# Column-norm attention and two MoE layers: three shared buffers, a shorter norm sum, and a new plan for the first groups

## Chip, cores and metric

One core of one Trainium2 chip. The metric is the device time of one execution in microseconds, the median of several runs. The engines are TensorE (PE: matmuls; PEld: its weight loads), VectorE (DVE), ScalarE (ACT), GpSimd (POOL, hardly used here) and SyncE (SP), which issues every DMA of this kernel.

## The reference

Cut to what matters (6016 tokens, 256 channels, hidden width 2048):

```python
qn = q / (np.linalg.norm(q, axis=1, keepdims=True) + 1e-06)   # norms over the 6016 tokens
kn = k / (np.linalg.norm(k, axis=1, keepdims=True) + 1e-06)
s = kn.transpose(0, 2, 1) @ qn / tau                          # 256 x 256
a = np.exp(s - s.max(-1, keepdims=True))
a /= a.sum(-1, keepdims=True) + 1e-09
x = v @ a                                                     # 6016 x 256
g = np.maximum(x @ w_in1, 0.0) ** 2;  x = g @ w_out1          # first layer
h = x @ w_in2
g = np.maximum(0.01 * h, h);          out = g @ w_out2        # second layer
```

All of it is in 32-bit floats. The weights reach the kernel as 64-bit numbers, which it converts itself.

## The kernel before, in words

**Splitting.** A product in full precision is made from three matmuls: each operand is split into a rounded high part and a low part (`split`, `low`, L137 to L142), and high x high, high x low and low x high are summed in PSUM (`mm3`, L572).

**Attention (L344 to L533).** q and k are read in 14 groups of 1, 2, ten times 4, 3 and 1 row tiles, five groups ahead. For each tile, TensorE accumulates the transposed scores `sT` (L423). For the norms, ScalarE squares a group (`square`, L386) and VectorE adds the squares of the groups of four into `acc` (`accumulate`, L400); after the last of them it adds `acc`'s four parts into `sums_`. The squares of the last two groups (3 and 1 tiles) are not added. At the end, `norm_sums` (L373) lets TensorE sum over partitions with matmuls of one column, four for each 512 columns: three times for the last-but-one group, once for `sums_`, once for the last group. A matmul of 32-bit floats shows as two records. From `pn` follow the norms (square root on ScalarE, a chain of small instructions on VectorE), the scaled scores `sTs`, their transposes `s`, maximum and exponential, the transposed exponentials `eT` with their split, and then `fold(0)`. `keep_warm` puts matmuls without a use between these.

**Fold (L270).** The first layer's input weights are multiplied by the attention matrix once, so that v itself can be the layer's input: `fold(g)` is 12 matmuls into bank `c`; `fold_high` (ScalarE) and `fold_low` (VectorE) scale and split the result into the tile `wi` of group g.

**Weights (`Unit`, L156).** A unit is 256 rows or columns of one weight matrix. Its steps are load (SP), exponent (VectorE), rebias (ScalarE), mantissa, mantissa_low, sign, high (VectorE), round (ScalarE), low (VectorE), store (SP). `first_i` are w_in's units 0 and 1, `first_o` is w_out's unit 0, `others` the rest of the first layer. In the attention the generators `steps_i` and `steps_o` hand out VectorE's steps one by one (`run`); the steps of ScalarE and the last subtraction are collected in `later` and put out where `flush(ACT)` or `flush(DVE)` stands.

**Layers.** The tokens are six blocks p of two halves of 512 (one of 448); the hidden width is eight groups g of 256. Group by group, `first` or `product` makes the hidden values, relu and square (or the leaky form) and the cast are ScalarE's, the low part is VectorE's, and `second` adds the product with w_out to the block's outputs `y`. Block 0 of layer 1 uses the function `plain`, all others `strassen`. After a block, `y_done` copies the two halves of `y` into a buffer `o` (`take`) and sends it off (`put`): to DRAM for the second layer, or to the output. `o` has one buffer in layer 1 (tag "o") and shares the two of `v` in layer 2 (tag "v"). `load_v` (L247) reads a half block of v in four DMAs.

**Order.** Every engine works strictly in the order in which its instructions are written. In the attention that order is the program's. After it, a planner collects `(time, function)` pairs in `plan` and writes them out sorted by time (L980). One plan unit is a matmul of 512 columns. `at` sets a time, `on` also reserves an engine, `fit` takes the first gap of an engine that is long enough (`Gaps`). The times of the first groups are in `PLAIN`, one dictionary each: `first`, `relu`, `square`, `cast`, `low`, `fold`, `fold_high`, `fold_low` and `second` are times from the group's start, `length` is the time to the next group, and `stretch` multiplies the times. The third dictionary holds for group 2 and all later groups of `plain`. `convert` (L829) fits the remaining weight units into the gaps.

Of the kernel before, what the change touches and what calls it, by code (L numbers as in the profile page):

```python
# [50 lines left out]
def attn_moe_moe2(  # L51
# [40 lines left out]
    def in_order(x):  # L92
        return x.rearrange("p (q k c) -> p k q c", q=Q, k=KC)

    def ordered(x):
        return x.rearrange("p (k q c) -> p k q c", q=Q, k=KC)
# [1 line left out]
    const = ctx.enter_context(tc.tile_pool(name="const", bufs=1))  # L98
    wpool = ctx.enter_context(tc.tile_pool(name="wpool", bufs=2))
    cpool = ctx.enter_context(tc.tile_pool(name="cpool", bufs=2))  # L100
    vpool = ctx.enter_context(tc.tile_pool(name="vpool", bufs=2))
    xpool = ctx.enter_context(tc.tile_pool(name="xpool", bufs=2))
    dram = ctx.enter_context(tc.tile_pool(name="dram", bufs=1, space=DRAM))
    ps_h = ctx.enter_context(tc.tile_pool(name="ps_h", bufs=1, space=PSUM))
# [210 lines left out]
    def flush(engine):  # L315
        steps, later[engine] = later[engine], []
        for step in steps:
            step()
# [18 lines left out]
    def run(steps, n):  # L337
        for _ in range(n):
            next(steps, None)
# [4 lines left out]
    with (  # L344
# [28 lines left out]
        def norm_sums(src, first=False, last=False):  # L373

            for b in range(4):
                x = src[:, b * P : (b + 1) * P]
                nc.tensor.matmul(  # L377
                    pn[:, b : b + 1], x, ones, start=first and b == 0, stop=last, skip_group_check=True
                )
# [6 lines left out]
        def square(n, t):  # L386
            g = groups[n][1]
            flat = t.rearrange("p g a c -> p g (a c)")
            if n == whole[0]:
                nc.scalar.activation(acc, flat, AF.Square)  # L390
                return
            squares[n] = att2.tile([P, G, 2 * C], F32, tag="sq", name="sq")
            if n <= whole[-1]:
                nc.scalar.activation(squares[n][:, :g], flat[:, :g], AF.Square)
                return
            nc.scalar.activation(squares[n][:, :g, :C], flat[:, :g, :C], AF.Square)
            for i in range(g):
                nc.scalar.activation(ordered(squares[n][:, i, C:]), in_order(flat[:, i, C:]), AF.Square)

        def accumulate(n):  # L400
            if not whole[0] <= n <= whole[-1]:
                return
            for i, at in ((0, 0), (1, 1)) if n == whole[0] else ((n, 0),):
                sq, g = squares.pop(i), groups[i][1]
                tt(acc[:, at : at + g], acc[:, at : at + g], sq[:, :g], op=ALU.add)
            if n == whole[-1]:
                tt(acc[:, 0:2], acc[:, 0:2], acc[:, 2:4], op=ALU.add)
                a0, a1 = acc[:, 0], acc[:, 1]
                tt(sums_[:, :C], a0[:, :C], a1[:, :C], op=ALU.add)
                tt(ordered(sums_[:, C:]), in_order(a0[:, C:]), in_order(a1[:, C:]), op=ALU.add)  # L410

        for n, (t0, g) in enumerate(groups):
            t = qk.pop(n)
            last_group = n == NS - 1
            flush(ACT)
            square(n, t)
            if last_group:
                nc.scalar.activation(small[:, 7, 0:1], ones, AF.Sqrt)
            accumulate(n - 1)
            flush(DVE)  # L420
            for i in reversed(range(g)):
                for j in range(KC):
                    nc.tensor.matmul(  # L423
                        sT[j][:, :C],
                        t[:, i, 0, j * P : (j + 1) * P],
                        t[:, i, 1],
                        start=n == 0 and i == g - 1,
                        stop=last_group and i == 0,
                    )
            if n == 1:  # L430
                for u in first_i:
                    u.load()
            if W0 <= n < W0 + 4:
                run(steps_i, 2)
            elif W0 + 4 <= n < W0 + 6:
                run(steps_i, 1)
            if n + AHEAD < NS:
                load_qk(n + AHEAD)
            elif n + AHEAD == NS:
                load_v(0, 0)  # L440
                first_o.load()
                nc.sync.dma_start(tau_sb, tau.partition_broadcast(P))
                load_v(0, 1)
            if n == W0 + 7:
                for u in others[:2]:
                    u.load()
        for i in range(3):
            norm_sums(squares[NS - 2][:, i], first=i == 0)
        norm_sums(sums_)
        norm_sums(squares[NS - 1][:, 0], last=True)  # L450
        run(steps_o, 2)
        flush(ACT)
        nc.vector.reciprocal(rtau, tau_sb)
        y, m, z, r = (small[:, i] for i in range(4))
        nc.scalar.activation(y, pn[:, :4], AF.Sqrt, bias=tiny, scale=0.25)
# [11 lines left out]
        sTs = [att.tile([P, C], F32, name=f"sTs{j}") for j in range(KC)]  # L467
        ts(ordered(sTs[0]), in_order(sT[0][:, :C]), r[:, 0:1], rtau, op0=ALU.mult, op1=ALU.mult)
        nc.scalar.activation(ordered(sTs[1]), in_order(sT[1][:, :C]), AF.Copy, scale=rq1)
        run(steps_o, 1)  # L470
        s = [bank("e", "s0"), bank("y3", "s1")]

        xs = att2.tile([P, 4, 512], F32, tag="sq", name="xs")
# [21 lines left out]
        for i in range(KC):  # L495
            nc.vector.reduce_max(mx[:, i], s[i][:, :C], axis=AX.X)
            ts(nb[:, i], mx[:, i], rk[:, i : i + 1], -1.0, op0=ALU.mult, op1=ALU.mult)
            nc.scalar.activation(
                e[i], s[i][:, :C], AF.Exp, bias=nb[:, i], scale=rk[:, i : i + 1], accum_out=sm[:, i]
            )  # L500
        x_transpose(0, 0)
        x_transpose(1, 0)
        for i in range(KC):
# [23 lines left out]
        x_high(2)  # L527
        x_low(1)
        x_low(2)
        run(steps_o, 3)  # L530
        flush(ACT)
        flush(DVE)
        first_o.store()  # L533


    gpool = ctx.enter_context(tc.tile_pool(name="gpool", bufs=4))
# [13 lines left out]
    def fit(engine, t, cost, fn, *args):  # L550
# [6 lines left out]


    PLAIN = [
        dict(first=(0, 6, 18.4, 24.4), fold=12, second=(), length=36, relu=(6.4, 12.4, 26.9, 34.2), stretch=1,  # L560
             square=(18, 36.9), cast=(29.6, 44.4), low=(34.7, 49.5), fold_high=22.6, fold_low=27),
        dict(first=(0, 6, 12, 18), fold=24, length=50, relu=(5.6, 13, 20.4, 30.6), stretch=1,
             second=((30.4, (1, 0, 0)), (36.4, (1, 0, 1)), (42.4, (1, 1, 0))),
             square=(15.7, 37.6), cast=(26, 42.2), low=(31.1, 47), fold_high=33.3, fold_low=39),
        dict(first=(0, 12, 30.4, 42.4), fold=24, length=62, stretch=1.14, relu=(6.4, 18.4, 36.8, 48.8),
             second=((6, (2, 1, 1)), (18, (1, 0, 0)), (36.4, (1, 0, 1)), (48.4, (1, 1, 0))),
             square=(21.2, 51.6), cast=(25.4, 55.8), low=(30.2, 60.6), fold_high=31, fold_low=37),
# [36 lines left out]
    def y_done(t, n, half):  # L604

        L, p, _ = units[n]
        w = WIDTH[p]
        key = L, p, half
        if key == (2, NP - 1, 1):
            at(t, finish_last)  # L610
            return
        o = {}

        def take(d):
            ys = y_t[key]
            if d == 0:

                o[0] = vpool.tile([P, 16, C // Q], F32, name="o", **({"tag": "v"} if L == 2 else {"tag": "o", "bufs": 1}))
            if L == 2:
                nc.vector.transpose(  # L620
                    o[0][:, : w // B, d * B : (d + 1) * B], ys[d][:, :w].rearrange("p (g t) -> p g t", t=B)
                )
                return
            to = o[0].rearrange("p g c -> p (g c)")[:, d * w : (d + 1) * w]
            (nc.scalar.copy if d == 0 else nc.vector.tensor_copy)(to, ys[d][:, :w])

        def put():
            if L == 2:
                for b, to in enumerate(blocked(out, p, half)):
                    nc.sync.dma_start(to, o[0][b * B : (b + 1) * B, : w // B])  # L630
                return
            for d in range(KC):
                from_ = o[0].rearrange("p g c -> p (g c)")[:, d * w : (d + 1) * w]
                nc.sync.dma_start(x2_d[p][:, SLOT[d, half], :w], from_)

        t0 = fit(DVE if L == 2 else ACT, t, 3.1 if L == 2 else 2.7, take, 0)
        t1 = fit(DVE, max(t, t0 - 3) if L == 1 else t0 - 0.5, 3.1, take, 1)
        at(max(t0, t1), put)
# [42 lines left out]
    def plain(n, t0):  # L681

        L, p, g = units[n]
        w = WIDTH[p]
        m = PLAIN[min(n, 2)]
        T = lambda x: t0 + m["stretch"] * x
        x_at = {(0, 0): (2, 0), (0, 1): (2, 1), (1, 1): (1, 0), (1, 0): (1, 1)}

# [116 lines left out]
    start, lengths, now = [], [], 0  # L805
    for n in range(LAST + 1):
        L, p, g = units[n] = n // (NP * NG) + 1, n // NG % NP, n % NG
        lengths.append(PLAIN[min(n, 2)]["length"] if n < NG else 45 * (WIDTH[p] + 32) / 544)
        start.append(now)
        now += lengths[-1]  # L810

    for n in range(LAST + 1):
        (plain if n < NG else strassen)(n, start[n])

# [51 lines left out]
    for i, u in enumerate(others):  # L866
        end = convert(u, 0, i < 2)
        n, x = (u.g - 1, "fold") if u.kind == "i" else (u.g + 1, "second")
        m = PLAIN[min(n, 2)]
        due = start[n] + m["stretch"] * (m[x] if u.kind == "i" else 18)  # L870
        assert end < due, (u.kind, u.g, end, due)
        if u.kind == "i":
            used["whl"][-1] = due + 8
# [139 lines left out]
```

## Time and profile before

| | |
|---|---|
| median of 3 runs | 1063.73 us (1063.1 to 1064.23) |
| profiled execution, its own time | 1062.22 us |
| its span, first to last instruction | 1060.3 us |
| TensorE busy | 1042.3 us, 98% of the span |
| VectorE, ScalarE busy | 786.8 us (74%), 715.8 us (68%) |
| mean granted clock of TensorE | 0.994 of 2.4 GHz |

Times in the trace count from the start of the span. Matmuls are pipelined and their ends are modelled, so a group's end can lie after the start of the next. A busy share is a mean over stages with different limits; what counts is which wait ends last in a stage.

### The profile page before, as it was taken

To read this page: it belongs to the slowest core of one execution; us is meant where nothing else is said; L and a number is where in the kernel's file an instruction comes from. 1 tells how busy PE (TensorE), PEld (TensorE's weight loads), DVE (VectorE), ACT (ScalarE), POOL (GpSimd) and SP (SyncE) were. 2 spreads that over 40 slices of the span, in tenths; PEclk is the share of its full clock that TensorE was granted. 3 is DMA by queue.
4 is the path that set the end of the run, shared out by engine and by line. 5 is a ranking of instruction groups with operands and counts; after the bars stand their busy time and mean duration, and the time that the engine had idled before them with its cause. 6 is when DMAs were issued, how large, how long until landed. Compare 5 with 4: busy or idle time off the path is not lost.

```text
span 1060.3 us, 12864 instructions
## 1 busy us (share of the span) xinstructions
PE 1042.3 (98%) x4798; PEld 881.1 (83%) x4798; DVE 786.8 (74%) x1096; ACT 715.8 (68%) x854; POOL 0.7 (0%) x6
## 2 busy tenths in 40 slices
PE   8989999999999999999998999999999999999998
PEld 6978888888888788998887888888888888998887
DVE  4788988887988888888886756866765765866554
ACT  5568887888888887887886655655655654655543
POOL 0000000000000000000000000000000000000000
PEclk9989999999999999999999999999999999999999
DMA  9937548558558658758466435544543634644431
GB/s 330 275 116 201 185 164 207 180 208 196 222 218 260 226 202 267 225 223 312 155 223 243 148 130 197 160 160 181 172 164 147 200 138 175 203 164 158 152 147 40
DMA packets 118590, 203.48 MB, mean 192 GB/s; under 512 B 52608, under 2 KB 66176, under 8 KB 116864
## 3 DMA queue, kind: packets, MB, share of 16 engines
q1 hardware_dynamic: 118528, 202.66, 56.6%
q8 instruction: 38, 0.62, 0.2%
q14 instruction: 24, 0.20, 0.1%
HBM read 165.15 MB, written 37.49 MB: 191 GB/s over the span
## 4 chain that ended last, share of the span: by engine, by line
PE 92%; DMA 3%; DVE 2%; issue 1%; SPq 1%; ACT 1%; DVEq 0%; ACTq 0%
PE y L574 43%; PE hc L574 11%; PE ha L574 10%; PE hb L574 10%; PE he L574 5%; PE sT L423 4%; PE h L574 4%; PE y L592 2%; DMA v<-in_v_dram 1%; DMA x<-o 1%; PE pw L278 1%; DVE c L763 1%; PE pn L377 1%; PE warm L135 0%; DMA wst<-in_moe_w_in_dram 0%
## 5 line engine op out<-in xcount | busy, mean ns | idle before, releaser
L574 PE MATMUL y<-g,wo 128*128 128x512 f32 (+1 forms) x2208 | 551.6, 385 | 0.0
L574 PEld LDWEIGHTS y<-g,wo 128*128 128x128 f32 x2208 | 414.6, 188 | 77.3
L138 DVE TENSOR_TENSOR g<-c,g 128x1024 fp32r<-128x1024 f32 (+1 forms) x192 | 230.4, 1200 | 28.0 <-ACT g L662 22.3
L662 ACT CAST g<-c 128x1024 fp32r<-128x1024 f32 (+1 forms) x192 | 198.8, 1035 | 4.5
L671 ACT ACTIVATE c<-c 128x1024 f32<-128x1024 f32 (+1 forms) x96 | 100.3, 1045 | 141.0 <-DVE c L763 141.0
L574 PE MATMUL hc<-x,wi 128*128 128x512 f32 (+1 forms) x528 | 146.7, 386 | 5.0 <-DVE c L763 4.9
L574 PE MATMUL hb<-x,wi 128*128 128x512 f32 (+1 forms) x528 | 146.6, 386 | 0.3 <-DVE c L763 0.3
L574 PE MATMUL ha<-x,wi 128*128 128x512 f32 (+1 forms) x528 | 146.9, 387 | 0.0
L574 PEld LDWEIGHTS hc<-x,wi 128*128 128x128 f32 x528 | 98.6, 188 | 25.1 <-DVE c L763 7.2
L574 PEld LDWEIGHTS hb<-x,wi 128*128 128x128 f32 x528 | 99.5, 189 | 19.3 <-DVE c L763 0.8
L574 PEld LDWEIGHTS ha<-x,wi 128*128 128x128 f32 x528 | 98.8, 189 | 17.6
L667 ACT ACTIVATE c<-c 128x1024 f32<-128x1024 f32 (+1 forms) x80 | 83.2, 1040 | 43.8 <-DVE c L763 43.6
L763 DVE TENSOR_TENSOR c<-u,hc 128x512 f32<-128x512 f32 (+1 forms) x88 | 59.5, 676 | 59.6 <-PE hc L574 58.9
L669 ACT ACTIVATE c<-c 128x1024 f32<-128x1024 f32 (+1 forms) x96 | 100.4, 1045 | 1.7
L763 DVE TENSOR_TENSOR c<-c,hb 128x512 f32<-128x512 f32 (+1 forms) x88 | 59.2, 672 | 52.1 <-PE hb L574 48.8
L763 DVE TENSOR_TENSOR c<-w,hc 128x512 f32<-128x512 f32 (+1 forms) x88 | 59.3, 674 | 45.3 <-PE hc L574 44.7
L752 ACT COPY u<-ha 128x512 f32<-128x512 f32 (+1 forms) x88 | 50.9, 578 | 58.7 <-PE ha L574 56.3
L763 DVE TENSOR_TENSOR w<-u,he 128x512 f32<-128x512 f32 (+1 forms) x88 | 59.1, 672 | 36.5 <-PE he L574 31.2
L574 PE MATMUL he<-x,wi 128*128 128x512 f32 (+1 forms) x264 | 73.0, 385 | 0.0
L763 DVE TENSOR_TENSOR c<-w,hb 128x512 f32<-128x512 f32 (+1 forms) x88 | 59.4, 675 | 9.5 <-DVE w L763 0.5
L752 ACT COPY c<-ha 128x512 f32<-128x512 f32 (+1 forms) x88 | 50.8, 577 | 20.3 <-PE ha L574 19.9
L574 PEld LDWEIGHTS he<-x,wi 128*128 128x128 f32 x264 | 49.6, 188 | 9.3
(98 smaller groups left out, 726.0 us busy)
## 6 DMA issues: line engine op xcount, KB each, us to landing
wi<-wi SPq DMA_DIRECT2D x80, 896.0 KB, 4.9
wo<-wo SPq DMA_DIRECT2D x96, 512.0 KB, 5.7
wi<-wi SPq DMA_DIRECT2D x24, 512.0 KB, 3.5
wst<-in_moe_w_in_dram SPq DMA_DIRECT2D x16, 512.0 KB, 5.6
wst<-in_moe_w_out_dram SPq DMA_DIRECT2D x16, 512.0 KB, 4.9
wi<-wis SPq DMA_DIRECT2D x8, 1024.0 KB, 4.7
qk<-in_q_dram SPq DMA_DIRECT2D x10, 512.0 KB, 7.9
qk<-in_k_dram SPq DMA_DIRECT2D x10, 512.0 KB, 8.3
```

What stands on the lines that cost most here:

```text
L138: tt(lo, x, raw(hi), op=ALU.subtract)
L278: nc.tensor.matmul(pw[:, i * 2 * P : (i + 1) * 2 * P], eT[j][a][:, i * P : (i + 1) * P], whl[g][:, b, j], start=t == 0 and i == 0, stop=t ...
L377: nc.tensor.matmul(pn[:, b : b + 1], x, ones, start=first and b == 0, stop=last, skip_group_check=True)
L423: nc.tensor.matmul(sT[j][:, :C], t[:, i, 0, j * P : (j + 1) * P], t[:, i, 1], start=n == 0 and i == g - 1, stop=last_group and i == 0,)
L574: nc.tensor.matmul(ps, a[m], b[n], start=first and i == 0, stop=last and i == 2, skip_group_check=True)
L592: nc.tensor.matmul(ys[t // 2][:, t % 2 * C : (t % 2 + 1) * C], gt[:, a, fb, t * P : (t + 1) * P], wo[:, b, :, fb], start=first and m == 0 ...
L662: nc.scalar.copy(g_t[n, half][:, 0, :, :w], c)
L667: nc.scalar.activation(c, c, AF.Relu)
L669: nc.scalar.activation(c, c, AF.Square)
L671: nc.scalar.activation(c, c, AF.Prelu, alpha=0.01)
L752: nc.scalar.copy(to, h_t[n, tag][:, :w])
L763: tt(to, x, h_t[n, tag][:, :w], op=ALU.add)
```

## The change

- The pool of v gets three buffers; the outputs `o` of both layers take theirs from it, in turn with v. The separate tag "o" goes.
- The squares of the last-but-one group are made in their natural order in one instruction; VectorE adds their three parts to `acc` (two additions of 512 columns, the last one into `sums_` in two halves). `acc`'s last addition covers all 512 columns. `norm_sums` is called for the last group and `sums_` only, in this order.
- w_out's unit 0: exponent, mantissa and mantissa_low stand after the last-but-one group's matmuls, sign and high after `norm_sums`, round after `sTs`, low after the exponentials, and the store there. Nothing of it is left at the attention's end.
- `PLAIN` has four dictionaries: three for groups 0, 1, 2 and the old third one for the rest. The order of relus, squares, casts and folds in them is new, and so are the gaps for the conversion. VectorE's first 14 units of the plan are reserved.

```diff
-    vpool = ctx.enter_context(tc.tile_pool(name="vpool", bufs=2))
+    vpool = ctx.enter_context(tc.tile_pool(name="vpool", bufs=3))
...
-            if n <= whole[-1]:
+            if n < NS - 1:
                 nc.scalar.activation(squares[n][:, :g], flat[:, :g], AF.Square)
                 return
-            nc.scalar.activation(squares[n][:, :g, :C], flat[:, :g, :C], AF.Square)
-            for i in range(g):
-                nc.scalar.activation(ordered(squares[n][:, i, C:]), in_order(flat[:, i, C:]), AF.Square)
+
+            last = squares[n][:, 0]
+            nc.scalar.activation(last[:, :C], flat[:, 0, :C], AF.Square)
+            nc.scalar.activation(ordered(last[:, C:]), in_order(flat[:, 0, C:]), AF.Square)
...
-                a0, a1 = acc[:, 0], acc[:, 1]
-                tt(sums_[:, :C], a0[:, :C], a1[:, :C], op=ALU.add)
-                tt(ordered(sums_[:, C:]), in_order(a0[:, C:]), in_order(a1[:, C:]), op=ALU.add)
+                tt(acc[:, 0], acc[:, 0], acc[:, 1], op=ALU.add)
...
+            if last_group:
+                sq, a = squares[n - 1], acc[:, 0]
+                for i in range(2):
+                    tt(a, a, sq[:, i], op=ALU.add)
+                tt(sums_[:, :C], a[:, :C], sq[:, 2, :C], op=ALU.add)
+                tt(ordered(sums_[:, C:]), in_order(a[:, C:]), in_order(sq[:, 2, C:]), op=ALU.add)
             flush(DVE)
...
-            if n == W0 + 7:
+            if n == NS - 2:
                 for u in others[:2]:
                     u.load()
-        for i in range(3):
-            norm_sums(squares[NS - 2][:, i], first=i == 0)
-        norm_sums(sums_)
-        norm_sums(squares[NS - 1][:, 0], last=True)
+                run(steps_o, 3)
+        norm_sums(squares[NS - 1][:, 0], first=True)
+        norm_sums(sums_, last=True)
         run(steps_o, 2)
-        flush(ACT)
...
-        run(steps_o, 1)
+        flush(ACT)
         s = [bank("e", "s0"), bank("y3", "s1")]
...
+        flush(DVE)
+        first_o.store()
         x_transpose(0, 0)
...
-        run(steps_o, 3)
-        flush(ACT)
-        flush(DVE)
-        first_o.store()
...
     PLAIN = [
-        dict(first=(0, 6, 18.4, 24.4), fold=12, second=(), length=36, relu=(6.4, 12.4, 26.9, 34.2), stretch=1,
-             square=(18, 36.9), cast=(29.6, 44.4), low=(34.7, 49.5), fold_high=22.6, fold_low=27),
-        dict(first=(0, 6, 12, 18), fold=24, length=50, relu=(5.6, 13, 20.4, 30.6), stretch=1,
-             second=((30.4, (1, 0, 0)), (36.4, (1, 0, 1)), (42.4, (1, 1, 0))),
-             square=(15.7, 37.6), cast=(26, 42.2), low=(31.1, 47), fold_high=33.3, fold_low=39),
+        dict(first=(0, 6, 18.4, 24.4), fold=12, second=(), length=30.4, relu=(6.4, 12.4, 24.9, 36.3), stretch=1,
+             square=(27.6, 49.3), cast=(39, 56.7), low=(44, 61.7), fold_high=19.2, fold_low=21.6),
+        dict(first=(0, 6, 12, 18), fold=30, length=60, relu=(16.1, 23.6, 33.9, 36.6), stretch=1,
+             second=((24, (1, 0, 0)), (36.4, (1, 0, 1)), (42.4, (1, 1, 0))),
+             square=(43.6, 52.8), cast=(48.2, 59.5), low=(53.3, 64.6), fold_high=39.3, fold_low=42),
+        dict(first=(0, 12, 24, 36), fold=42, length=67, stretch=1.14, relu=(6.4, 18.4, 30.4, 42.4),
+             second=((6, (2, 1, 1)), (18, (1, 0, 0)), (30, (1, 0, 1)), (48.4, (1, 1, 0))),
+             square=(21.2, 53.2), cast=(25.4, 57.4), low=(30.2, 62), fold_high=48.8, fold_low=53.5),
         dict(first=(0, 12, 30.4, 42.4), fold=24, length=62, stretch=1.14, relu=(6.4, 18.4, 36.8, 48.8),
...
-                o[0] = vpool.tile([P, 16, C // Q], F32, name="o", **({"tag": "v"} if L == 2 else {"tag": "o", "bufs": 1}))
+                o[0] = vpool.tile([P, 16, C // Q], F32, tag="v", name="o")
...
-        m = PLAIN[min(n, 2)]
+        m = PLAIN[min(n, 3)]
...
+    DVE.take(0, 14)
```

## Rows read from the trace of the kernel before

**Rows 1.** Windows: stretch, length, busy per engine, granted clock, DMA share, GB/s.

```profile
50.00:60.00 10.00, 9.97 (x61) 9.68 (x60) 4.87 (x18) 3.66 (x10) 0.00 (x0) 0.66 0.02 7
...
100.00:120.00 20.00, 20.00 (x101) 17.03 (x100) 19.01 (x34) 16.71 (x26) 0.00 (x0) 1.00 0.51 173
...
400.00:600.00 200.00, 195.57 (x890) 167.69 (x890) 162.15 (x233) 156.83 (x186) 0.00 (x0) 0.99 0.65 227
```

**Rows 2.** Timeline of TensorE, 46 to 82 us: start, duration, what [idle before, releaser].

```profile
48.39 2.73 PE L377 MATMUL pn<-ones,sq 128*128 128x1 f32 x24
50.99 1.38 PE L377 MATMUL pn<-ones,sums 128*128 128x1 f32 x8
52.23 1.85 PE L377 MATMUL pn<-ones,sq 128*128 128x1 f32 x8
...
60.11 1.89 PE L278 MATMUL pw<-whl,eT 128*128 128x256 f32 x12
62.56 0.73 PE L574 MATMUL h<-x,wi 128*128 128x512 f32 x2 [0.56 <-ACT wi L296]
...
70.12 1.66 PE L574 MATMUL h<-x,wi 128*128 128x512 f32 x6 [1.29 <-ACT c L700]
73.25 0.73 PE L574 MATMUL h<-x,wi 128*128 128x512 f32 x2 [1.46 <-ACT wi L296]
...
80.74 1.55 PE L574 MATMUL y<-g,wo 128*128 128x512 f32 x6
```

**Rows 3.** Chain of waits in order of time, undisturbed stretch: start, duration, what.

```profile
101.44 1.36 PE y L574 x6
102.81 1.43 PE pw L278 x12
```

**Rows 4.** Timeline of VectorE, 28 to 64 us.

```profile
44.93 0.42 DVE L409 TENSOR_TENSOR sums<-acc 128x256 f32<-128x256 f32 x1
...
45.61 0.42 DVE L174 TENSOR_SCALAR ce<-wst 128x512 uint32<-128x512 uint32 x1
...
60.09 0.76 DVE L138 TENSOR_TENSOR eT<-eT,eT 128x256 fp32r<-128x256 f32 x2
```

**Rows 5.** Timeline of all engines, 55 to 110 us: the attention's end.

```profile
67.15 0.62 ACT L223 CAST wo<-cm 128x512 fp32r<-128x512 f32 x1 [2.09 <-DVE cm L196]
...
67.80 0.69 DVE L138 TENSOR_TENSOR wo<-cm,wo 128x512 fp32r<-128x512 f32 x1 [0.69 <-ACT wo L223]
...
68.87 0.72 ACT L177 ACTIVATE ce<-ce,rebias 128x512 uint32<-128x512 uint32 x1 [1.09 <-DVE ce L174]
...
69.50 1.06 ACT L700 ACTIVATE c<-h 128x512 f32<-128x512 f32 x2
```

**Rows 6.** Who waited for whom, whole span: us in total, times, longest.

```profile
ACT o L625 <- DMA x<-o: 15.6, 5, 5.5
...
PE hc L574 <- DVE c L763: 4.9, 3, 3.4
```

**Rows 7.** Timeline of all engines, 566 to 586 us.

```profile
578.69 0.59 ACT L625 COPY o<-y 128x512 f32<-128x512 f32 x1 [5.48 <-DMA x<-o]
...
582.52 0.96 PE L574 MATMUL hc<-x,wi 128*128 128x512 f32 x3 [3.41 <-DVE c L763]
```

**Rows 8.** Windows behind that wait; columns as in rows 1.

```profile
584.00:586.00 2.00, 2.00 (x6) 1.60 (x5) 1.35 (x2) 1.35 (x2) 0.00 (x0) 0.50 0.44 108
```

**Rows 9.** Timeline of TensorE, 582 to 596 us: the 16th matmul.

```profile
587.66 1.52 PE L574 MATMUL y<-g,wo 128*128 128x512 f32 x6
```

**Rows 10.** Timeline of TensorE, 486 to 500 us.

```profile
497.11 0.97 PE L574 MATMUL hc<-x,wi 128*128 128x512 f32 x3 [0.98 <-DVE c L763]
```

**Rows 11.** Timelines of SP and ScalarE, 413 to 430 us.

```profile
414.84 0.80 SPq L634 DMA_DIRECT2D x<-o  x2
...
416.22 9.31 SPq L251 DMA_DIRECT2D v<-in_v_dram  x8
...
420.71 0.59 ACT L625 COPY o<-y 128x512 f32<-128x512 f32 x1 [2.86 <-DMA x<-o]
```

More of the change, by code (lines that the diff above doesn't have):

```diff
@@ L807, in attn_moe_moe2 @@
         L, p, g = units[n] = n // (NP * NG) + 1, n // NG % NP, n % NG
-        lengths.append(PLAIN[min(n, 2)]["length"] if n < NG else 45 * (WIDTH[p] + 32) / 544)
+        lengths.append(PLAIN[min(n, 3)]["length"] if n < NG else 45 * (WIDTH[p] + 32) / 544)
         start.append(now)
         now += lengths[-1]
+    DVE.take(0, 14)
     for n in range(LAST + 1):
@@ L868, in attn_moe_moe2 @@
         n, x = (u.g - 1, "fold") if u.kind == "i" else (u.g + 1, "second")
-        m = PLAIN[min(n, 2)]
+        m = PLAIN[min(n, 3)]
         due = start[n] + m["stretch"] * (m[x] if u.kind == "i" else 18)
```

## The prediction

> **What bounds the kernel now.** I read the page first. TensorE is busy 98% of the span (the table above), so only time in which TensorE waits, or does work that need not be done, can be won. The windows say where that is: one stretch around 50 us in which the granted clock has a mean of 0.66, and a loss of 4.4 us somewhere in 400 to 600; at 100 to 120 TensorE is full, and the vector engine with 19.0 of 20 us nearly so [rows 1]. The timeline of TensorE from 46 to 82 us then gives the places of the first loss [rows 2]: matmuls with one column (pn) hold it from 48.39 to 54.07, and between the first folded group (62.56) and 80.74 it waits three times in the listed pieces. The chain of waits gives the price of undisturbed work: six matmuls of 512 columns in 1.36 us (0.227 each), a fold in 1.43 [rows 3]. The table of waits shows what is behind the second loss: three waits of TensorE for `c`, 4.9 us in all, and beside them ScalarE waiting 15.6 us for the DMA that empties the one output buffer [rows 6].
>
> **Part 1: squares of the last-but-one group.** Before, TensorE sums 20 column blocks; each is two records, so 24 (last-but-one group) + 8 + 8. The first 24 take 48.39 to 50.99, 0.108 us each [rows 2]. The change takes exactly these away. The remaining 16 need 16 x 0.108 = 1.73, so pn would end near 50.2 instead of 54.07: 3.8 us. That is more than the 2.60 of the 24, because the last 8 of before ran at half clock (1.85 for 8, from 52.23) [rows 2]. The 0.66 of the window means 6.8 us at 1.2 GHz [rows 1]. If the 16 ran at that rate throughout, they would need 3.7 and the gain would be 2.0. I take 3.8, since records slow down only within the eight from 50.99 (about 51.5), and keep 2.0 as the other end.
>
> What VectorE takes over must be there when the last group's 8 records are through, at 48.39 + 0.87 = 49.26. Its queue is free for it at 44.93, after the additions of the whole groups [rows 4]. Two additions of 256 columns start 0.34 apart there (44.93 to 45.61 for two), so a listed 0.42 costs 0.34, and a 512-column instruction listed at 0.69 [rows 5] about 0.62. In order: one addition in place of the two short ones (0.62), exponent, mantissa and low mantissa of w_out's first rows (0.34 + 0.34 + 0.62; the weights had landed by 45.61, where the exponent starts without a wait [rows 4]), two additions of 512 (1.24), two of 256 (0.68): 44.93 + 3.84 = 48.77. With listed times, nothing overlapped, it is 49.37. So the cover holds by 0.5 us or misses by 0.1. Sign and high follow (1.24), done near 50.0 to 50.8, behind pn's end and the square root; they cost 0 to 0.3. On ScalarE the rebias now stands ahead of the last group's squares and waits for the exponent near 46; those squares are then done well before 48.39.
>
> **Part 2: the conversion's end between scores and softmax.** Rounding on ScalarE stands in its wait for the scores. The subtraction (0.69 [rows 5]) now stands on VectorE ahead of the v transposes. VectorE is without a listed wait there until eT's subtraction at 60.09 [rows 4], and the fold needs that, as the first group needs what VectorE does next. I put 0.5 of the 0.69 on the path; 0 if a gap takes it. Parts 1 and 2 together: -3.8 + 0.5 = -3.3, from -3.8 (nothing paid) to -1.0 (2.0 gained, 0.69 and 0.3 paid).
>
> **Part 3: the end of the attention and the new plan.** Before, the rounding of w_out waits on ScalarE until 67.15 for VectorE, the rebias of the next weights until 68.87, and so the first relu, whose matmuls were long done, runs at 69.50 [rows 5]. It frees the bank for which TensorE stands still until 70.12; then fold_high is late and TensorE waits to 73.25 [rows 2]. From 62.56 to 80.74 TensorE has 48 matmuls and two folds, 48 x 0.227 + 2 x 1.43 = 13.8 us; it takes 18.2. Of the 4.4 lost, about 0.55 stays (the first fold_low). 3.8 can be won.
>
> I walked the new order with the durations of the rows and the times of before; ScalarE comes free of v's casts at 65.0, VectorE of their low parts at 65.8, 1.6 to 2.7 before it was free of w_out. ScalarE: relu at 65.0 and 66.0, rebias, fold_high at 67.5 and 67.9, relu 68.8. VectorE: fold_low done at 68.8, sign, high. TensorE: group 1 starts at 70.0 without a wait. The nearest approach is group 1's fourth product at 74.1, which needs a relu that ends at 73.7. Then second(0,0,0) at 75.5, fold(2) at 76.8, group 2 at 81.0: nothing waits. In the third group fold(3) stands at plan time 42 of 67, and only one product of 1.36 us lies between it and group 3. In my walk ScalarE reaches that fold_high at 93.0 (a rounding ahead of it waits 0.9 for VectorE), fold_low comes 1.3 later, and TensorE waits 1.1 us. The tight place is mine from the order; the queues there are as full as rows 1 show. I take -3.8 + 0.9 = -2.9: bounds -3.8 (no wait) and -1.9 (a wait of 1.9, if both engines are late by another rounding). From group 4 on, the plan's order is the old one, shifted.
>
> **Part 4: three shared buffers.** Before, the second output of a block could not be copied before the first one's DMA had landed: ScalarE waits 5.5 us up to 578.69, everything behind it is late, and TensorE stands 3.41 us until 582.52 [rows 7]. After this the clock is 0.50 in 584 to 586 [rows 8], and the 15 matmuls from 582.52 to 587.66 take 5.14 instead of 3.41 [rows 7, 9]: another 1.73. In the same way 0.98 before 497.11 [rows 10]. With three buffers in turn, the second output takes the buffer of a v block that was transposed half a block of work ago; these waits go: -3.41 - 1.73 - 0.98 = -6.1. Bounds: -4.4 (the clock falls anyway, and a part is lost elsewhere) to -6.6 (the third wait of rows 6 goes too; its cause, as I read the queue, is a late v load, so I leave it).
> The Trainium skill (TensorE: Matmul & The Clock Gate, "HAM oscillation — how this bites in real kernels") states that a gap in the matmul stream drops the gate and the matmuls behind it run cold. By that rule a gap costs more than its length; the trace agrees with 1.73 us behind 3.41, and without it the sum would be 1.7 smaller.
>
> What pays for it: load_v of the second half now needs the DMA of the first output, and this wait stands on SP, ahead of the weight loads. Outputs are issued at 414.84 and land by 420.71, where ScalarE's wait ends; the eight v issues run from 416.22 for 9.31 us, so the second four come at about 420.9 [rows 11]. The wait is 0 to 0.2, and its half of v is transposed microseconds later. I cost it at nothing; without that cover one block pays what the landing takes longer.
>
> **Sum.** -3.3 - 2.9 - 6.1 = -12.3. The profiled execution took 1062.22, so 1049.9; the median of the runs, 1063.73, lies 1.5 above it, and against that it is 1051.4. With every bound at its own end the sum is -14.2 (3.8 + 3.8 + 6.6) to -7.3 (1.0 + 1.9 + 4.4): 1049.5 to 1056.4 against the median.
>
> **Rivals.**
> *A. The outputs' wait goes, but TensorE stops at the same places for something else* (a late v load, as in the third wait). For it: ScalarE waited in five blocks and TensorE suffered in two or three [rows 6]. Against: at 582.52 nothing else is late. Time 1051.4 + 6.1 = 1057.5.
> *B. VectorE is the bound of the groups after the attention.* 19.0 of 20 us busy [rows 1]; work pulled forward leaves it no slack and part 3 is given back later. Against: three of its instructions move ahead of 62.56. Time 1051.4 + 2.9 = 1054.3.
> *C. The half-rate stretch moves into useful work.* In before its 6.8 us fell on pn, fillers and transposes, and was over before the fold at 60.11 [rows 2]. The fold now starts near 60.11 - 3.8 + 0.5 = 56.8. If the whole stretch fell on folds and first products, it would cost 3.4: 1054.8. If it stays at its place (51.5 to 58.3) it reaches 1.5 us into the fold: 0.75, hidden in part by VectorE.
> [...]
> *D. Slower: the shared ring blocks SP.* Four v loads stand behind an output's DMA. If this landed late, weight loads and DMAs behind it are late, and TensorE waits at each of four block ends. To eat 12.3 us each must cost over 3.1 us of TensorE, though weights are loaded two groups (some 20 us) ahead; the landing of 5.9 us would have to become more than 20. Time above 1066.
> The Trainium skill (DMA: Bandwidth & Descriptors, "Two DMAs through the same engine are not ordered") states that only the completion semaphore orders such DMAs, so the wait must stand at the issuing engine; rows 11 show it at 0 to 0.2 us.
> *E. It does nothing:* every saved wait returns at the next queue, near 1063.
>
> **How the numbers follow.** Forecast 0.62, A 0.10, B 0.12, C 0.10, D 0.03, E 0.03. The predicted time is the likeliest case, 1051.4. The range 1048.5 to 1057.5 takes in A, B, C and the bounds, with 1 us below for the spread of runs. A measurement of this kernel tells apart about 0.2% (2 us). Faster by more: 0.62 + 0.10 + 0.12 + 0.10 = 0.94; the same 0.03 (E); slower 0.03 (D).
>
> **What would show it.** Part 1: 16 pn records that end 3.8 us earlier without a wait between the 8 and the 8. Part 2: eT's subtraction half a microsecond further behind the scores. Part 3: no wait of TensorE up to group 3, one of about 1 us there. Part 4: no ScalarE wait on L625, no drop of the clock near 580. I am wrong if pn's second 8 wait for the additions, if the wait before group 3 is several microseconds, or if SP stands long at the v loads.

## The result, and the profile after

The changed kernel takes 1048.97 us (median of 4 runs, 1048.34 to 1049.83); the kernel before, run beside it, 1063.98 (4 runs, 1063.1 to 1067.12). The ratio is 0.9854, 95% interval 0.9832 to 0.9876: about 15 us or 1.5% faster. The prediction's direction and places hold, but 0.9854 of the 1063.73 it was made against is 1048.2, just below its range, which starts at 1048.5. The edge itself is within the noise: the interval gives 1045.9 to 1050.5, and by the medians the same figure is 1048.7 (the ratio lies near that of the means, in which the execution of 1067.12 counts in full). The profiled execution of after took 1049.60 (span 1047.8), 12.6 less than that of before; predicted were 12.3.

The starts of four matmuls in the trace divide each span: the first `pn` record, the first product of block 0 (`h`), the first `hc` of layer 1, and the last matmul.

| us | to pn | pn to h | h to hc | hc to last | span |
|---|---|---|---|---|---|
| before | 48.39 | 14.17 | 101.00 | 891.73 | 1060.3 |
| after | 48.59 | 11.56 | 98.41 | 884.27 | 1047.8 |
| difference | +0.2 | -2.6 | -2.6 | -7.5 | -12.5 |
| predicted | 0 | -3.3 (parts 1, 2) | -2.9 (part 3) | -6.1 (part 4) | -12.3 |

Windows of after, to set beside [rows 1], columns the same:

```profile
50.00:60.00 10.00, 8.45 (x54) 7.85 (x54) 8.55 (x27) 5.92 (x15) 0.00 (x0) 0.83 0.17 67
100.00:120.00 20.00, 20.00 (x95) 16.81 (x94) 19.13 (x32) 16.77 (x26) 0.00 (x0) 1.00 0.53 185
400.00:600.00 200.00, 200.00 (x921) 172.49 (x920) 166.98 (x238) 160.12 (x189) 0.00 (x0) 1.00 0.66 229
```

TensorE is now full for all of 400 to 600, at a granted clock of 1.00; the stretch around 50 us still has half clock, 3.4 us of it instead of 6.8. TensorE's timeline of after, beside [rows 2]:

```profile
48.59 0.95 PE L377 MATMUL pn<-ones,sq 128*128 128x1 f32 x8
49.87 1.05 PE L377 MATMUL pn<-ones,sums 128*128 128x1 f32 x8 [0.33 <-DVE sums L423]
...
53.06 1.02 PE L492 MATMUL s<-ident,sTs 128*128 128x128 f32 x4 [1.14 <-DVE sTs L471]
53.87 3.04 PE L135 MATMUL warm<-ident 128*128 128x128 f32 x14
56.75 0.60 PE L515 MATMUL eT<-ident,e 128*128 128x128 f32 x4
...
60.15 0.73 PE L578 MATMUL h<-x,wi 128*128 128x512 f32 x2 [0.56 <-ACT wi L296]
61.03 2.57 PE L578 MATMUL h<-x,wi 128*128 128x512 f32 x10 [0.15 <-DVE wi L299]
63.44 1.60 PE L278 MATMUL pw<-whl,eT 128*128 128x256 f32 x12
64.87 8.35 PE L578 MATMUL h<-x,wi 128*128 128x512 f32 x36
73.06 1.52 PE L578 MATMUL y<-g,wo 128*128 128x512 f32 x6
...
91.17 0.73 PE L578 MATMUL h<-x,wi 128*128 128x512 f32 x2
92.52 1.19 PE L578 MATMUL h<-x,wi 128*128 128x512 f32 x4 [0.62 <-DVE wi L299]
```

The 24 records of the last-but-one group are gone, and the second eight wait 0.33 for VectorE's additions. 36 products now run from 64.87 without a wait, where before stood still twice. The new wait is at group 3: from 91.17 to 92.52 two matmuls (0.45) and 0.90 of loss, 1.1 with the gap of 0.23 ahead of 91.17. VectorE at the attention's end, beside [rows 4]:

```profile
46.54 0.43 DVE L174 TENSOR_SCALAR ce<-wst 128x512 uint32<-128x512 uint32 x1 [0.50 <-DMA wst<-in_moe_w_out_dram]
...
47.95 1.41 DVE L422 TENSOR_TENSOR acc<-acc,sq 128x512 f32<-128x512 f32 x2
49.39 0.42 DVE L423 TENSOR_TENSOR sums<-acc,sq 128x256 f32<-128x256 f32 x1
...
55.08 0.68 DVE L138 TENSOR_TENSOR wo<-cm,wo 128x512 fp32r<-128x512 f32 x1
...
57.68 0.76 DVE L138 TENSOR_TENSOR eT<-eT,eT 128x256 fp32r<-128x256 f32 x2 [0.23 <-ACT eT L141]
```

The exponent now waits 0.50 for the weights' DMA, which in this execution lands near 46.5 (in before by 45.61), and that half microsecond is what the additions are late by. Waits of after, beside [rows 6]:

```profile
PE h L578 <- DVE wi L299: 0.8, 2, 0.6
...
PE hc L578 <- DVE c L766: 0.5, 1, 0.5
...
PE hb L578 <- DVE c L766: 0.2, 1, 0.2
```

and one of SP's:

```profile
SPq L251 <- DMA x<-o: 2.3, 3, 1.0
```

ScalarE's 15.6 us for the output buffer no longer occur, and TensorE's waits for `c`, 4.9 us at `hc` [rows 6] and 0.3 at `hb` in before, are 0.5 and 0.2 (near 345 and 340 us). The price is where the prediction looked for it, on SP at the v loads: 2.3 us in three waits, the longest 1.0, and no wait of TensorE is followed back to it: it stands ahead of a block's second four v loads, and the late load near 339 us is one of the first four.

### The profile page after: what moved, and what is told of

The parts are those of the page before. It is cut to its first block, busy times and chain, and to the rows that moved or that the text cites. A ratio compares the mean times of both kernels' runs of the same rounds, so it can differ in the third digit from the quotient of the medians.

```text
span 1047.8 us, 12812 instructions
## 1 busy us (share of the span) xinstructions
PE 1034.5 (99%) x4774; PEld 876.2 (84%) x4774; DVE 789.1 (75%) x1099; ACT 716.4 (68%) x851; POOL 0.7 (0%) x6
## 4 chain that ended last, share of the span: by engine, by line
PE 93%; DVE 2%; DMA 2%; SPq 1%; ACT 1%; issue 0%; DVEq 0%; ACTq 0%
PE y L578 45%; PE hc L578 11%; PE ha L578 11%; PE hb L578 11%; PE he L578 5%; PE h L578 4%; PE sT L428 2%; PE y L596 2%; PE pw L278 1%; DMA qk<-in_k_dram 1%; SPq L251 1%; DMA wst<-in_moe_w_out_dram 1%; DMA v<-in_v_dram 1%; DVE g L138 0%; PE warm L135 0%
```

## The experiments

All ratios are against the kernel before, run beside each on the same chip (its medians there are 1063.89 to 1064.32); a difference in us is one of medians.

**Each part alone.** `ring_only` is before with the first and sixth piece of the diff (three buffers, tag "v"):

```diff
-    vpool = ctx.enter_context(tc.tile_pool(name="vpool", bufs=2))
+    vpool = ctx.enter_context(tc.tile_pool(name="vpool", bufs=3))
...
-                o[0] = vpool.tile([P, 16, C // Q], F32, name="o", **({"tag": "v"} if L == 2 else {"tag": "o", "bufs": 1}))
+                o[0] = vpool.tile([P, 16, C // Q], F32, tag="v", name="o")
```

`attn_only` is before with all pieces inside the attention (squares, `norm_sums`, `run` and `flush`); `plan_only` is before with the new `PLAIN`, its index and `DVE.take`.

> The kernel before with the three shared buffers alone. Theory 1 (the part of the gain that the sum missed lies in the buffers: in most runs of before, the wait for the output's DMA and the clock behind it cost more than in its profiled execution): 8.5 to 10 us faster than before, about 1054.5. Theory 2 (the missed part lies in the attention's end): 7 us faster, about 1057, which is what the profiled execution of before loses at its waits for c from 260 us on. Both: no ScalarE wait for the DMA of x<-o, no half clock near 580 us. Rival A of the prediction (TensorE stops there for something else): about 1063.

> The kernel before with the attention's edits alone (last-but-one squares on VectorE, w_out's first rows converted earlier), old plan, old buffers. Theory 1: the first product starts 2.4 us earlier, as in the changed kernel's trace, and the first relu no longer stands behind w_out's rounding, which gives 1 to 1.5 more: 3.5 to 4 us faster, about 1060. Theory 2: 6 us faster, 1058, since the runs of before lose more here than its profile shows.

> The kernel before with the new plan of three groups and VectorE's reserved first 14 units alone. Both theories: w_out's rounding still stands ahead of the first relu on ScalarE, so TensorE waits there; the fold is cast earlier, so 0.5 to 2 us faster than before, about 1062.5. If the plan's gain needs the attention's edits, no gain at all: 1064.

Measured: `ring_only` 1055.91, ratio 0.9924 (0.9911 to 0.9937), -8.0 us. `attn_only` 1057.17, 0.9932 (0.9918 to 0.9947), -6.7. `plan_only` 1061.71, 0.9981 (0.9967 to 0.9995), -2.2. TensorE's timeline of `attn_only`:

```profile
58.68 0.73 PE L575 MATMUL h<-x,wi 128*128 128x512 f32 x2 [0.56 <-ACT wi L296]
...
66.65 0.73 PE L575 MATMUL h<-x,wi 128*128 128x512 f32 x2 [0.32 <-ACT wi L296]
67.54 5.27 PE L575 MATMUL h<-x,wi 128*128 128x512 f32 x22 [0.15 <-DVE wi L299]
```

and of `plan_only`:

```profile
73.75 1.65 PE L577 MATMUL h<-x,wi 128*128 128x512 f32 x6 [0.29 <-ACT c L703]
75.79 1.65 PE L577 MATMUL h<-x,wi 128*128 128x512 f32 x6 [0.39 <-ACT c L703]
...
96.74 1.19 PE L577 MATMUL h<-x,wi 128*128 128x512 f32 x4 [0.62 <-DVE wi L299]
```

With the old plan and the moved conversion, the wait of 1.29 before 70.12 [rows 2] is gone and that of 1.46 before 73.25 is 0.32 (the 0.15 behind it was 0.19 in before). The new plan without the moved conversion keeps 0.29 and 0.39 there and adds the wait before group 3. The two are cures of one illness, and the conversion is the better one; so the three parts alone add up to 16.9 us, more than the 15.0 of the whole.

**Each part undone.** `ring_undone` is after with two buffers and tag "o" again; `plan_undone` is after with the old `PLAIN`, its old index and without `DVE.take`.

```diff
-        m = PLAIN[min(n, 3)]
+        m = PLAIN[min(n, 2)]
...
-    DVE.take(0, 14)
```

> The changed kernel with the old buffers (two for v, one for the first layer's outputs, all else as changed). Theory 1: 8.5 to 10 us slower than the changed kernel, about 1058, and the wait of TensorE near 570 us of varying length. Theory 2: 7 us slower, 1056. If the parts help each other, less than the sum of the three.

> The changed kernel with the old plan of two groups and without the reserved units: the attention's edits and the three buffers alone. Theory P (the prediction's part 3: the new plan is what takes away TensorE's waits after the attention): 2 to 3.8 us slower than the changed kernel, 1051 to 1053. Theory Q (w_out's rounding, moved out of the way by the attention's edits, was the cause of these waits, and the new plan only exchanges a wait of about 1 us ahead of group 1 for one of about 1.1 ahead of group 3): no difference, 1048.5 to 1049.5.

Measured: `ring_undone` 1056.45, 0.9924 (0.9912 to 0.9936); `plan_undone` 1050.44, 0.9874 (0.9854 to 0.9893). The buffers are thus worth 7.5 in after. The plan is worth 1.5 by the medians and perhaps nothing: the intervals of after and `plan_undone` overlap, and from h to hc they take 98.41 and 98.24. A wait and a window of `ring_undone`:

```profile
575.25 0.96 PE L578 MATMUL hc<-x,wi 128*128 128x512 f32 x3 [3.38 <-DVE c L766]
```

```profile
577.00:579.00 2.00, 2.00 (x6) 1.57 (x5) 1.08 (x1) 1.08 (x2) 0.00 (x0) 0.50 0.60 165
```

With the old buffers the wait of [rows 7] and the half clock of [rows 8] are back, at the same place of the work.

**The attention's edits divided.** `conv_only` is before with w_out's conversion moved (the `run`, `flush` and `store` lines); `norm_only` has the squares, the additions and the two `norm_sums` calls alone.

> The kernel before with nothing but w_out's first rows converted earlier (the squares of the last-but-one group still on TensorE, old plan, old buffers). Theory Q (the three waits between 62.56 and 74 come from w_out's rounding on ScalarE, and in a part of the executions a half clock follows them): the first product starts 0.3 to 0.5 later than in before, the waits shrink from 4.2 to 1 us, and the kernel is 2.5 to 4.5 us faster than before, about 1060.5. Theory P (the plan is needed for it): no faster, 1063.5 to 1064.5.

> Only the additions of the last-but-one group's squares on VectorE and the shorter sums on TensorE; w_out's conversion stays at its old place. If the two halves of the attention edits add up (-6.7 for both, -2.4 for the conversion alone) this gives about -4.3, ratio 0.996, with the three waits of TensorE near 66 to 72 us still there (about 4 us in all). If the sums' gain is only TensorE's 2.6 us of records, it is -2.6, ratio 0.9975.

Measured: `conv_only` 1061.44, 0.9973 (0.9962 to 0.9984), -2.4; `norm_only` 1060.24, 0.9961 (0.9944 to 0.9978), -3.9. Together they make -6.4 (-7.0 by the ratios), against -6.7 (-7.2) for both in `attn_only`: the halves add up. `norm_only` keeps the waits of before:

```profile
59.71 0.73 PE L577 MATMUL h<-x,wi 128*128 128x512 f32 x2 [0.56 <-ACT wi L296]
...
67.26 1.67 PE L577 MATMUL h<-x,wi 128*128 128x512 f32 x6 [1.28 <-ACT c L702]
70.39 0.73 PE L577 MATMUL h<-x,wi 128*128 128x512 f32 x2 [1.46 <-ACT wi L296]
```

and in `conv_only` the first is gone and the second is 0.35:

```profile
71.78 0.73 PE L572 MATMUL h<-x,wi 128*128 128x512 f32 x2 [0.35 <-ACT wi L296]
```

From h to hc, `conv_only` takes 98.25, `norm_only` 101.04, before 101.00: the moved conversion alone gives all that part 3 gains.

**What is left around 50 us.** `sums_first` is after with the additions ahead of all conversion; `low_later` is after with w_out's last subtraction and its store back at the attention's end; `fillers_2` is after with fewer matmuls without a use behind `s`.

```diff
# sums_first
                     u.load()
-                run(steps_o, 3)
         norm_sums(squares[NS - 1][:, 0], first=True)
         norm_sums(sums_, last=True)
+        run(steps_o, 3)
+        flush(ACT)
# low_later
-        flush(DVE)
-        first_o.store()
         x_transpose(0, 0)
...
         x_low(2)
+        flush(DVE)
+        first_o.store()
# fillers_2
-        keep_warm(warm, 6)
+        keep_warm(warm, 2)
```

> The changed kernel with VectorE's additions of the squares ahead of all conversion of w_out, whose weights land late in some executions. The last 8 norm matmuls then wait for nothing (0.3 to 0.7 us in the profiles of the changed order): 0.3 to 0.7 faster, about 1048.4, and the first product earlier by as much. Rival: sign and high then end later than the square root and the chain of small instructions pays it back: no difference.

> The changed kernel with the last subtraction of w_out's first rows (and the store) moved from behind the exponentials to the attention's end. If it stands on the path, as part 2 has it: eT's subtraction comes 0.5 us earlier and the kernel is 0.3 to 0.5 faster, 1048.5. Rival: in executions in which the clock is at half around the scores, TensorE's fillers hold the transposes of e longer than VectorE does, and it gives nothing there: 0 to 0.2. Either way too little for the interval; the traces tell.

> The changed kernel with two instead of six filler matmuls between the transposes of the scores and those of e. If the fillers at half clock stand on the path (they took 3.0 us in the changed kernel's profile, and the transposes of e started behind them 0.9 us after e was there): up to 0.9 us faster in executions with half clock there, 0 in the others; about 1048.5. Rival: fewer fillers let the clock fall more often or for longer, into the fold and the first products: 0.5 to 2 us slower.

Measured: `sums_first` 1049.27, 0.9864 (0.985 to 0.9879); `low_later` 1049.64, 0.9868 (0.9843 to 0.9892); `fillers_2` 1050.31, 0.9876 (0.9855 to 0.9898). None can be told from after: the intervals overlap. The traces still tell something. TensorE's timeline of `sums_first`:

```profile
49.54 1.03 PE L377 MATMUL pn<-ones,sums 128*128 128x1 f32 x8
...
53.30 1.73 PE L135 MATMUL warm<-ident 128*128 128x128 f32 x14
...
57.32 1.43 PE L278 MATMUL pw<-whl,eT 128*128 128x256 f32 x8 [0.30 <-DVE eT L138]
59.32 3.00 PE L579 MATMUL h<-x,wi 128*128 128x512 f32 x10 [0.56 <-ACT wi L296]
```

The second eight follow the first without a wait; no half clock shows here, and the 14 fillers take 1.73 instead of the 3.04 of after. From pn to h it is 10.6 us instead of 11.6. The edit is not shown to be the cause: `ring_undone` and `v_early`, whose attention is that of after, show no half clock there either and take 10.5 and 10.7. The fillers of `v_early`:

```profile
53.29 1.73 PE L135 MATMUL warm<-ident 128*128 128x128 f32 x14
```

In all three the fold, no longer behind slow fillers, waits 0.30 for `eT`. `low_later` has the half clock (52.4 for 3.4 us) and takes 11.7: behind slow fillers, VectorE's subtraction cost nothing in this one execution. `fillers_2` takes 11.6 as well, though its second eight wait 0.61: the half clock then lies on the transposes too.

**The last late v load.** `v_early` is after with the first half of v read ten plan units sooner from block 2 of layer 1 on; `best_b` is `v_early`, `sums_first` and `low_later` in one.

```diff
-            at(t0 + 62, load_v, p, 0)
+            at(t0 + (52 if p > 1 else 62), load_v, p, 0)
```

> The changed kernel with the first half block of v loaded at plan time 52 instead of 62 after a block's start (from block 2 on). If the remaining waits near 340 us (0.2 to 2.0 us in the profiles so far, with a half clock behind the longest) come from VectorE's wait for this load: they go, at least the first of the two; 0.5 to 1.5 us faster, 1048, and a narrower spread. Rival: the load now meets the output's DMA and the weights, and lands no earlier: no difference.

> The changed kernel with three edits: squares added first, the last subtraction of w_out at the attention's end, v's first half loaded earlier. If the three add: 1 to 2 us faster than the changed kernel, 1047 to 1048. If the attention's chain is held by the fillers at half clock and the v load lands no earlier: 1048.5 to 1049.

Measured: `v_early` 1047.58 (1047.57 to 1048.06), 0.9848 (0.9834 to 0.9862); `best_b` 1047.46 (1047.19 to 1049.91), 0.9851 (0.9835 to 0.9867). Both medians are lower than that of after, by 1.4 and 1.5, but the intervals of the ratios overlap with after's, so a gain over after is not shown. VectorE ahead of TensorE's wait at 340.56 in after:

```profile
339.29 0.65 DVE L255 STREAM_TRANSPOSE xr<-v 128x448 f32<-128x448 f32 x1 [2.53 <-DMA v<-in_v_dram]
```

In `v_early` no transposition waits for v, and TensorE has no wait near 340 or 345; from hc to the last matmul it takes 883.19 against 884.27. In the profiled execution of `fillers_2` the same load was later still:

```profile
342.60 0.96 PE L578 MATMUL hb<-x,wi 128*128 128x512 f32 x3 [1.86 <-DVE c L766]
343.40 2.57 PE L578 MATMUL y<-g,wo 128*128 128x512 f32 x6
```

The six behind it take 2.36 (343.40 to 345.76, where `hc` starts) instead of 1.36: half clock again. The execution took 1053.04, the slowest of its four. In `best_b`, pn to h takes 9.98: without half clock, the subtraction that `sums_first` still had there was worth 0.6.

**The kernel before, profiled again**, four times, without any edit.

> The kernel before once more, for a second profile. If its executions differ in the wait for the output's DMA (theory 1), this one has other waits for c than 0.21, 0.33, 0.48, 0.98 and 3.41 us, or another length of half clock behind them, and with a time near 1064 they are larger. If they differ in the attention (theory 2), the first product starts later than 62.56.

> The kernel before, profiled once more. If its executions differ at the attention's end as the first two did, about half of them show a stretch of half clock of 3.4 us right behind the three waits near 69 to 75 us (some 1.5 us dearer) and take 1064 or more; if the stretch in the second one was a single event, this one is like the first: no half clock there, 1062 to 1063 us.

> As for the second: a stretch of half clock behind the waits near 69 to 75 us and 1064 or more, or none and 1062 to 1063. By either theory the waits near 582 are 3.4 to 3.7 us with half clock behind them.

> As for the two before it. The times of the three together with their half-clock stretches say whether the number of such stretches orders the executions (1.5 to 1.7 us for each 3.4 us of half clock), or whether the spread comes from longer waits.

| us | own time | to pn | pn to h | h to hc | hc to last | half clock (start, length) |
|---|---|---|---|---|---|---|
| before | 1062.22 | 48.39 | 14.17 | 101.00 | 891.73 | 51.5, 6.8; 584.0, 3.4 |
| before_again | 1065.82 | 50.26 | 12.77 | 102.79 | 892.97 | 10.6, 3.4; 55.0, 3.4; 75.5, 3.4; 587.5, 3.4 |
| before_p2 | 1066.05 | 50.47 | 12.78 | 102.76 | 893.02 | 10.7, 3.4; 55.1, 3.4; 75.6, 3.4; 584.1, 6.8 |
| before_p3 | 1064.52 | 48.52 | 14.19 | 101.28 | 893.51 | 53.7, 6.8; 582.8, 6.8 |
| before_p4 | 1063.00 | 48.08 | 12.89 | 102.64 | 892.55 | 52.3, 3.4; 72.8, 3.4; 584.8, 3.4 |

Windows of `before_p2`: near 12 us, behind the attention, and behind the long wait:

```profile
11.00:14.00 3.00, 3.00 (x8) 2.38 (x8) 1.37 (x2) 2.13 (x2) 0.00 (x0) 0.50 1.09 385
588.00:590.00 2.00, 2.00 (x7) 1.52 (x6) 0.62 (x1) 0.58 (x1) 0.00 (x0) 0.50 0.76 271
```

```profile
76.00:78.00 2.00, 2.00 (x6) 1.60 (x5) 1.52 (x2) 1.97 (x4) 0.00 (x0) 0.50 0.72 240
```

The same work runs in each, but the stretches of half clock lie elsewhere. The guess with which these runs began, that a stretch behind the attention's waits makes an execution slow, falls: pn to h and h to hc together take 115.2 to 115.6 in all five. An execution either has 6.8 us of half clock ahead of h, or 3.4 there and 3.4 behind the waits. The spread is made elsewhere: 2 us by the half clock near 11 us, in two of five, and 0.8 to 1.8 between hc and the end. There it is the longer half clock behind the long wait in two (1.1 and 1.3), the waits near 265 and 340 us in `before_p4`, and in `before_again` for the most part something else: from about 428 to 480 us its matmuls of 448 columns start 0.207 apart instead of 0.203, at a granted clock of 1.00, about 1 us in all. The execution that the prediction was made from is the lowest of the five in that last column.

## Why the prediction was nearly right, and where it failed

**The step that failed is the last of the Sum:** "the median of the runs, 1063.73, lies 1.5 above it, and against that it is 1051.4". It carries over to the changed kernel what the executions of before have above the profiled one. After has nothing of the kind: its median, 1048.97, lies 0.6 below its profiled execution. So 12.6 between the profiles became 15.0 between the medians: 1.8 from before's median (1063.98) over its profile, 0.6 from after's under its own. Of the 3.2 between the 1051.4 and 1048.2, this step makes 2.4; 0.3 are the 12.6 for 12.3, and 0.5 is the ratio against the medians.

By the five profiles, before's part is made of longer half clock behind the wait near 580, of the waits near 265 and from 340 to 346, of the slower matmuls of `before_again`, and of the half clock near 11 us. The first goes with part 4's wait; the late v load and the slower matmuls stay possible in the changed kernel (`low_later` has both).

After's part has a trace of its own in the clock: its two executions of 1048.34 and 1048.35 have a mean granted clock of 0.999 and 1.000, the profiled one 0.998. They have no room for a stretch of 3.4 us at half clock, which alone takes 0.0016 off the mean, and without it the attention took about 1 us less in `ring_undone` and `v_early`. Of the half clock near 11 us, which stands ahead of everything changed, it stays open whether the changed kernel has it more seldom: three of the eight profiles with the longer sums have it (the third is `conv_only`), none of the ten with the shorter ones, and no run says why.

**That 12.3 and 12.6 agree is in part luck.** Parts 1 to 3 gave 1.0 less than their terms and part 4 gave 1.4 more.

**Part 4 was mis-sized:** 7.5 instead of 6.1 in the profiles, beyond its bound of 6.6. The start-to-start times give it: the wait at 582.52 and the half clock behind it cost 5.3 (predicted 5.1), the one at 497.11 1.25 (0.98), small waits near 267 and 430 0.7 (not counted, gone too), and 0.1 each near 346 and 508. A listed idle of 3.41 takes 3.68 out of the chain of starts. Against an execution with 6.8 us of half clock there it is more still, which fits the -8.0 of `ring_only`.

**Parts 1 and 2** gave 2.6 in the profiles (3.3 predicted). The second eight waited 0.33, since the weights landed later than in before, and 3.4 us of half clock fell on `s` and the fillers. In `attn_only` and `ring_undone`, whose eight do not wait, it is 3.5 and 3.7. The 3.8 of part 1 holds 1.2 for half clock on pn's records; that was an accident of the one execution, and the half clock only moves: `before_p3`, with none on pn, spends 4.5 us there instead of 5.7, and its first product comes no sooner (pn to h 14.19). That the subtraction costs half a microsecond is right at full clock (0.6, `best_b` against `sums_first`) and wrong behind slow fillers (0, `low_later` against after), each by one execution.

**Part 3's size holds** (2.6 for 2.9, group 3 waiting 1.1 as walked), **its cause only half.** The prediction gave the gain to the conversion and the plan together. The conversion alone brings it, and the plan trades a wait of 0.9 at the fold for one of 1.1 at group 3. How the gain divides between parts 1 and 2 and part 3 also hangs on which execution of before is taken: against the three with 3.4 us of half clock ahead of h it is 1.2 to 1.3 and 4.2 to 4.4, and only the sum (5.2 to 5.6, predicted 6.2) holds against all five.

**The rivals.** A came true in its smallest form: the one v load it named still stops TensorE, by 1.2 us in after (1.4 in before) and by 3.7, half clock included, in `fillers_2`; nothing else is late at 497 or 580. B is refuted: what part 3 gains by the early groups is still there at hc, and from 100 to 120 TensorE is full beside a VectorE that is busy 19.1 of 20 us. C: the half clock is there (53.2 to 56.6), but it ends ahead of the fold. D: SP waits, for 1.0 at most in after (1.8 in `low_later`), where the prediction had 0 to 0.2, and TensorE does not feel it. E is refuted.

## What to carry to other kernels

A forecast made against one profiled execution should be set against the median only after a second profile has shown what the other executions have more of; where that is half clock behind a wait, and the change removes the wait, the excess goes with it. A buffer that an output's DMA must leave before the next copy can stop TensorE an engine further on, and a third turn in an existing pool, at the price of 2.3 us of waits on SP, took all of it. When one change holds two cures for the same wait (work moved away and a new order around it), do each alone before crediting both.

## What the runs showed of the hardware

- In all 18 profiles half clock came in stretches of 3.4 or 6.8 us, but for those at the very end. In ten profiles with the old output buffers TensorE waits 3.3 to 3.5 us near 580; in six of them half clock for 3.4 us goes with it, in three for 6.8, and in one (`norm_only`) none. The Trainium skill (TensorE: Matmul & The Clock Gate, "HAM oscillation — how this bites in real kernels") says that matmuls behind a long enough wait for data start cold. The trace agrees for the long wait in nine of ten; the waits of 0.8 to 1.1 near 497 never did it, those of 1.3 to 1.5 near 340 (`ring_only`, `plan_undone`, `sums_first`, `conv_only`) did not, and one of 1.86 at the same place (`fillers_2`) did.
- A wait costs more than its listed idle. In before, 4.13 us lie between the last start ahead of the listed 3.41 (578.73) and the second start behind it (582.86), where two undisturbed steps take 0.45: 3.68 lost. The listed 0.98 is 1.25 by the same count.
- Fillers are not free when the clock is low: the same 14 took 1.73 us at full clock and 3.04 in after, and the transposes behind them started 3.7 us after the first of `s` instead of 2.1 (`sums_first`).
- How late a v load lands differs: VectorE's longest wait for one is 1.7 us in `before_p4`, 1.9 in before, 2.5 in after, 3.6 in `ring_only` and 4.2 in `fillers_2`, which all read it at the same place; ten plan units sooner took the wait away.
- Matmuls of the same shape can be slower at a granted clock of 1.00. In `before_again`, `plan_only` and `low_later` those of 448 columns in layer 1 start 0.207 apart for some 50 us between 420 and 482, in the other fifteen profiles 0.203 throughout; over some 250 of them that is about 1 us. No run shows the cause.
